# Two attentions with a gate on one core: reciprocals and V copies spread by DMA, taps along the free axis, slices unit by unit on GpSimd, the head in halves, a new order

## The chip, the cores and the metric

The kernel runs on one core of a Trainium2 chip. The metric is the device time of one execution in microseconds. Five engines run their own queues of instructions in order: TensorE (PE in the profile, PEld its weight loads), VectorE (DVE), ScalarE (ACT), GpSimd (POOL) and SyncE (SP), which here issues nearly all transfers (DMA). Semaphores order work between engines.

## The reference

Input x has 2048 tokens of 640 features. Two attention layers of 32 heads with 20 features each read the same x: A is full softmax attention, B looks at 8 earlier tokens, two apart. A gate mixes them.

```python
def _A_ref(x, wqkv, wo):            # H = 32, Dh = 20
    q, k, v = ...                   # (x @ wqkv) split by heads
    p = softmax(einsum("bhqd,bhkd->bhqk", q, k) * Dh ** -0.5)
    return einsum("bhqk,bhkd->bhqd", p, v) ... @ wo

def _B_ref(x, wqkv, wo):            # W, dil = 8, 2
    idx = pos[:, None] - (arange(W) * dil)[None, :]      # masked where negative
    logits = einsum("bhsd,bhswd->bhsw", q, kg) * scale   # kg, vg: k, v gathered by idx
    o = einsum("bhsw,bhswd->bhsd", softmax(logits), vg)
    return ... @ wo

x = A_x                             # B_x is not used
g = sigmoid((x * gate_w).sum(-1, keepdims=True))
return g * _A_ref(x, A_wqkv, A_wo) + (1 - g) * _B_ref(x, B_wqkv, B_wo)
```

## The kernel before, in words

**Units.** A's scores are computed transposed: 128 keys on the partitions, 512 queries along the free axis, for one head. Such a 128x512 block is a unit; four heads, 16 key blocks and 512 queries make a group of 64 units, and there are 32 groups, 2048 units. The sum with V, `pv` (L1868), collects a group in the PSUM bank `obank`, with the four heads in four strips of 32 partitions; V has a column of ones, so row 0 of each strip is the sum of the exponentials.

**Two routes for the exponential.** A tile of two or three units goes through `qk` (L1805, PE) into one of two PSUM tensors `score` and then through one ACT exponential of 1024 or 1536 columns, `exp` (L1823), into `ebuf`. Units of some key blocks (a quad of four heads, `dquads`) go another way: `clamp` (L1783) turns the scores into an int16 on DVE, `uD`, whose bits read as bf16 are a first power of two, and `gen_d` (L952) adds constants to it for three further slices `eD`; the four are summed by PE with weights that GpSimd has multiplied into V (`vS`, `gen_vs`, L972). A unit takes this route when the planner finds DVE free.

**B.** For 256 tokens at a time, `gen_bproj` makes q, k and v (`qkvB`), `gen_b` makes eight products of q with shifted k on DVE (L1064), some of them on GpSimd (L1055), and PE sums them over a head's features. The eight taps lie on partition strips of 32 and two halves of the free axis, so the maximum over the taps takes six small DVE steps on `mxB` (L1104 to L1116). ACT makes the exponential `eB` (L1121), `rQ` the reciprocal, which goes through DRAM (`scr_r`) to `rB`; V's shifted copies `vR` are 16 transfers for each 256 tokens (L1034); DVE and GpSimd multiply them (L1185, L1175).

**Normalising A.** When a group is complete, `gen_norm` transposes `obank` in blocks of 32 on DVE (L912), takes 16 reciprocals per partition (L916), GpSimd multiplies with the gate (L920) and with the transposed values (L929), DVE transposes back (L932), and DMAs carry the rows to `oTd`. `gen_fold` multiplies with the output weights.

**The order.** The kernel plans its own instruction order as Python code when it is built: `_Sched.task` (`T`) holds an estimated time for each engine, gives every step a cost, and sets the semaphores. Generators (`gens`) wait for a condition, for a PSUM bank, for DVE, for a GpSimd slot; the main loop takes a tile, then lets generators fill the time until the next exponential. `PLAN` holds the loop's parameters, by tile number. GpSimd steps wait for the last DVE step that is marked `port` and are placed where DVE is planned to read PSUM. What the planner decides stands as a fixed order in each queue; on the chip only the semaphores act.

**The head.** Four loads of 512 tokens of x, each followed by 20 transposes on PE (`turn`), a copy on ACT and one on DVE (`x_out`), then a projection of the first four heads' K (`k_first`), its maximum (`k_max`) and its copy (`k_out`); the first q needs all four maxima (`KM`). The last group's normalising and four output blocks make the tail.

Of the kernel before, what the change touches and what calls it, by code (L numbers as in the profile page):

```python
# [52 lines left out]
    0: ((0.334, 0.55), 0.25, 1.0, 5.5, 0.89, -1.23, -0.43, 12.02, 7.0, 4.65, 0.75, 0.51, 5.31, 4.81, -0.12, 0.35, 2, -1.5, 0.3, -1.0, (2, 2)),  # L53
    5: ((0.334, 0.55), 0.25, 1.0, 5.5, 0.96, -1.48, -0.43, 4.81, 7.0, 4.65, 0.71, 0.65, 4.56, 2.7, -0.12, 0.35, 2, -6, 0.3, -1.0, (2, 2)),
    10: ((0.334, 0.55), 0.2, 1.0, 5.5, 0.96, -1.48, -0.43, 4.81, 7.0, 10.07, 0.71, 0.65, 4.56, 2.7, -0.12, 0.35, 2, -7, 0.3, -1.0, (2, 2)),
    15: ((0.32, 0.76), 0.25, 1.0, 5.5, 0.96, -1.19, -0.43, 4.77, 7.0, 4.65, 0.75, 0.51, 5.31, 4.81, 0.0, 0.65, 1, -1.3, 0.3, -1.0, (2, 2)),
    20: ((0.38, 0.68), 0.25, 6.6, 5.5, 0.94, -1.26, -1.28, 4.81, 5.5, 6.07, 0.67, 0.54, 5.64, 3.94, 0.2, 0.68, 2, -1.5, 0.3, -1.0, (2, 2)),
    25: ((0.278, 0.677), 0.0, 3.02, 2.45, 0.84, -1.3, -0.51, 5.92, 2.0, 7.76, 0.35, 0.65, 5.31, 2.52, -0.06, 0.68, 2, -3.7, 0.3, -1.0, (2, 2)),
    30: ((0.261, 0.681), 0.11, 6.6, 5.5, 0.94, -1.48, -1.28, 4.81, 5.5, 8.05, 0.67, 0.54, 4.4, 3.94, 0.2, 0.68, 2, -1.5, 0.3, -1.0, (2, 2)),
    35: ((0.275, 0.615), 0.11, 6.6, 5.5, 0.94, -1.48, -1.28, 4.81, 5.5, 8.05, 0.67, 0.54, 4.4, 3.47, 0.2, 0.68, 2, -3, 0.3, -1.0, (2, 2)),  # L60
    40: ((0.261, 0.681), 0.11, 1.0, 2.5, 0.94, -1.48, -0.22, 11.8, 5.5, 8.05, 0.67, 0.54, 6.8, 4.42, 0.0, 0.68, 2, -3, 0.3, -1.0, (2, 2)),
    45: ((0.261, 0.681), 0.11, 1.0, 2.5, 0.94, -1.48, -0.22, 4.81, 2.96, 7.27, 0.67, 0.54, 6.8, 4.42, 0.0, 0.68, 2, -3, 0.3, -1.0, (2, 2)),
    50: ((0.34, 0.51), 0.39, 1.0, 5.5, 0.89, -1.26, -0.43, 7.8, 2.0, 4.65, 0.91, 0.18, 5.31, 4.07, 0.08, 0.59, 2, -1.5, 0.3, -1.0, (2, 2)),
    55: ((0.34, 0.546), 0.39, 1.0, 5.5, 0.89, -1.26, -0.43, 7.8, 2.0, 5.23, 0.91, 0.18, 5.31, 4.07, 0.08, 0.59, 2, -1.5, 0.3, -1.0, (2, 2)),
    60: ((0.412, 0.644), 0.39, 1.0, 6.06, 0.69, -1.26, -0.43, 7.8, 2.0, 4.65, 0.91, 0.32, 5.31, 4.07, 0.08, 0.59, 2, -1.5, 0.3, -1.0, (2, 2)),
    65: ((0.381, 0.757), 0.39, 1.0, 6.06, 0.69, -1.26, -0.43, 7.8, 2.0, 4.65, 0.91, 0.32, 5.31, 4.07, 0.08, 0.59, 2, -1.5, 0.3, -1.0, (2, 2)),
    75: ((0.381, 0.757), 0.39, 1.0, 6.06, 0.69, -1.26, -0.43, 7.8, 2.0, 4.65, 0.91, 0.2, 5.31, 4.07, 0.08, 0.59, 2, -1.5, 0.3, -1.0, (2, 2)),
    85: ((0.381, 0.757), 0.39, 1.0, 6.06, 0.69, -1.26, -2, 10.69, 1.53, 4.65, 0.91, 0.2, 5.31, 4.67, 0.08, 0.59, 2, -1.5, 0.3, -1.0, (2, 2)),
    90: ((0.381, 0.757), 0.39, 1, 6.06, 0.69, -1.26, -2, 10.69, 1.53, 4.65, 0.59, 0.2, 5.31, 4.67, 0.08, 0.63, 2, -1.5, 0.3, -1.0, (2, 2)),
    95: ((0.34, 0.51), 0.39, 1.0, 5.5, 0.89, -1.26, -0.43, 7.8, 2.0, 4.65, 0.91, 0.32, 5.31, 4.07, 0.08, 0.59, 2, -1.5, 0.3, -1.0, (2, 2)),  # L70
    100: ((0.34, 0.51), 0.39, 1, 1.0, 0.89, -1.26, -0.43, 7.8, 7.0, 7.54, 0.91, 0.32, 5.31, 4.07, 0.08, 0.59, 2, -1.5, 0.3, -1.0, (2, 2)),
    105: ((0.34, 0.51), 0.39, 1, 1.0, 0.89, -1.26, -1.38, 7.8, 7.0, 7.54, 0.91, 0.32, 5.31, 4.07, 0.08, 0.59, 2, -1.5, 0.3, -1.0, (2, 2)),
    110: ((0.412, 0.644), 0.39, 1.0, 1.0, 0.69, -1.6, -0.92, 7.8, 2.0, 4.68, 0.91, 0.54, 3.16, 4.29, 0.0, 0.65, 2, -2.77, 0.3, -1.0, (2, 2)),
    115: ((0.291, 0.715), 0.39, 1.0, 1.0, 0.94, -1.6, -0.92, 5.92, 2.0, 4.68, 0.64, 0.65, 4.56, 4.29, 0.0, 0.65, 2, -3, 0.3, -1.0, (2, 2)),
    120: ((0.336, 0.75), 0.33, 1.0, 1.0, 0.89, -1.06, -0.4, 5.92, 2.0, 9.17, 0.6, 0.65, 4.56, 4.74, 0.0, 0.65, 2, -6, 0.3, -1.0, (2, 2)),
    130: ((0.361, 0.799), 0.33, 1.0, 1.0, 1.21, -1.19, -0.4, 5.92, 2.0, 9.17, 0.6, 0.65, 4.56, 4.74, 0.03, 0.65, 2, -6, 0.3, -1.0, (2, 2)),
    135: ((0.361, 0.799), 0.33, 1.0, 1.0, 1.21, -0.99, -0.4, 5.92, 2.0, 9.17, 0.59, 0.65, 3.16, 4.74, 0.03, 0.69, 2, -6.83, 0.3, -1.0, (2, 2)),
    140: ((0.34, 0.51), 0.39, 1, 1.0, 0.89, -1.26, -0.43, 6.62, 1, 4.65, 0.57, 0.51, 5.56, 4.07, 0.05, 0.73, 1, -3, 0.3, -1.0, (2, 2)),
    145: ((0.34, 0.51), 0.39, 1, 1.0, 0.89, -1.26, -0.43, 6.62, 1.4, 4.73, 0.57, 0.51, 5.56, 4.07, 0.05, 0.73, 1, -3, 0.3, -1.0, (2, 2)),
    150: ((0.34, 0.51), 0.39, 1, 1.0, 0.89, -1.26, -0.43, 6.62, 1.4, 4.73, 0.68, 0.51, 5.56, 4.07, 0.05, 0.73, 1, -3, 0.3, -1.0, (2, 2)),  # L80
    155: ((0.224, 0.681), 0.33, 1, 1.0, 1.09, -1.48, -1.81, 3.55, 7.0, 7.19, 0.7, 0.65, 5.53, 3.9, 0.2, 0.72, 2, -3, 0.3, -1.0, (2, 2)),
    160: ((0.217, 0.576), 0.33, 1, 1.0, 1.23, -1.48, -1.81, 3.55, 7.0, 7.19, 0.7, 0.65, 5.53, 3.9, 0.2, 0.68, 2, -3, 0.3, -1.0, (2, 2)),
    165: ((0.217, 0.576), 0.33, 1, 1.0, 1.23, -1.48, -1.81, 3.55, 7.0, 7.19, 0.7, 0.75, 5.53, 3.9, 0.2, 0.68, 2, -3, 0.39, -1.0, (2, 2)),
    170: ((0.27, 0.431), 0.33, 1, 1.0, 1.23, -1.48, -1.81, 3.55, 7.0, 7.19, 0.7, 0.75, 5.53, 4.13, 0.2, 0.68, 2, -3, 0.39, -1.0, (2, 2)),
    175: ((0.224, 0.681), 0.33, 1.56, 1.0, 1.02, -1.48, -1.81, 3.55, 8, 7.19, 0.7, 0.65, 5.53, 3.31, 0.2, 0.57, 2, -3, 0.3, -1.0, (2, 2)),
    180: ((0.389, 0.582), 0.25, 2.5, 1.0, 1.02, -1.48, -1.81, 4.81, 6.7, 7.54, 0.7, 0.65, 5.64, 4.29, 0.0, 0.57, 2, -3, 0.3, -1.0, (2, 2)),
    185: ((0.389, 0.582), 0.25, 2.5, 1.0, 0.89, -1.48, -0.43, 6.62, 4.81, 7.54, 0.7, 0.2, 5.31, 4.07, 0.06, 0.59, 2, -3, 0.3, -1.0, (2, 2)),
    190: ((0.29, 0.69), 0.37, 1.56, 1.58, 1.23, -1.53, -1.81, 3.55, 2.0, 5.03, 0.56, 0.47, 5.53, 2.91, 0.2, 0.65, 1, -3, 0.3, -1.0, (2, 2)),
    195: ((0.29, 0.69), 0.35, 1.56, 1.58, 1.23, -1.34, -1.81, 2, 2.0, 5.03, 0.56, 0.47, 5.53, 2.91, 0.2, 0.65, 1, -3, 0.3, -1.0, (2, 2)),
    200: ((0.278, 0.663), 0.35, 1.56, 1.58, 1.23, -1.34, -1.81, 2, 2.0, 5.03, 0.56, 0.47, 5.53, 2.75, 0.2, 0.61, 1, -3, 0.3, -1.0, (2, 2)),  # L90
    205: ((0.278, 0.663), 0.35, 1.56, 1.58, 1.23, -1.34, -1.81, 2, 2.0, 5.03, 0.56, 0.5, 4.37, 2.75, 0.2, 0.61, 1, -3, 0.26, -1.0, (2, 2)),
    210: ((0.278, 0.663), 0.35, 1.56, 1.58, 1.23, -1.34, -1.81, 2, 2.0, 5.03, 0.56, 0.66, 4.37, 2.75, 0.2, 0.61, 1, -3, 0.26, -1.0, (2, 2)),
    215: ((0.274, 0.542), 0.35, 1.56, 1.58, 1.23, -1.34, -1.81, 2, 1, 8.57, 0.56, 0.66, 4.37, 2.75, 0.2, 0.68, 1, -3, 0.26, -1.0, (2, 2)),
    225: ((0.291, 0.715), 0.2, 1.56, 1.16, 1.23, -1.34, -1.81, 2, 1, 8.57, 0.56, 0.66, 4.37, 2.75, 0.2, 0.68, 1, -3, 0.08, -1.0, (2, 2)),
    230: ((0.29, 0.69), 0.16, 1.56, 1.0, 1.21, -0.76, -1.81, 2, 1, 8.57, 0.56, 0.59, 4.37, 3.61, 0.08, 0.73, 2, -3.49, 0.3, -1.0, (2, 2)),
    235: ((0.29, 0.69), 0.25, 3.79, 1.0, 1.37, -1.53, -0.8, 15.9, 2.0, 5.03, 0.56, 0.47, 3.16, 3.17, 0.2, 0.65, 1, -3, 0.3, -1.0, (2, 2)),
    240: ((0.34, 0.68), 0.38, 2.91, 1.0, 0.89, -1.79, -0.55, 4.03, 7.0, 5.03, 0.52, 0.58, 6.49, 4.57, 0.1, 0.73, 1, -4.31, 0.3, -1.0, (2, 2)),
    245: ((0.388, 0.773), 0.38, 2.91, 1.0, 0.89, -1.79, -0.55, 4.03, 7.0, 5.03, 0.52, 0.58, 4.56, 2.7, 0.1, 0.73, 1, -4.31, 0.3, -1.0, (2, 2)),
    250: ((0.388, 0.773), 0.38, 2.91, 1.0, 0.89, -1.79, -0.55, 4.03, 7.0, 5.03, 0.52, 0.58, 4.56, 2.7, 0.1, 0.67, 1, -4.31, 0.3, -1.0, (2, 2)),
    255: ((0.364, 0.476), 0.0, 1.0, 1.0, 1.21, -1.26, -0.52, 11.51, 2.0, 8.02, 0.83, 0.65, 3.16, 3.17, 0.0, 0.61, 2, -4.7, 0.3, -1.0, (2, 2)),  # L100
    260: ((0.364, 0.476), 0.0, 1.0, 1.0, 1.21, -1.26, -0.52, 11.51, 2.0, 7.91, 0.83, 0.36, 3.16, 3.17, 0.0, 0.61, 2, -4.7, 0.3, -1.0, (2, 2)),
    265: ((0.364, 0.476), 0.0, 1.0, 1.0, 1.21, -1.26, -0.52, 11.51, 6.7, 9.43, 0.83, 0.36, 3.16, 3.17, 0.0, 0.61, 2, -4.7, 0.3, -1.0, (0, 2)),
    270: ((0.364, 0.476), 0.16, 1.0, 1.0, 1.21, -1.26, -0.52, 11.51, 6.7, 9.43, 0.83, 0.36, 3.16, 3.17, 0.0, 0.61, 1, -4.7, 0.3, -1.0, (0, 2)),
    275: ((0.389, 0.582), 0.16, 1.0, 1.0, 1.21, -1.26, -0.52, 11.51, 6.7, 9.43, 0.83, 0.36, 3.16, 3.17, 0.0, 0.61, 1, -4.7, 0.3, -1.0, (0, 2)),
# [314 lines left out]
def _build(ctx, nc, A_x, A_wqkv, A_wo, B_wqkv, B_wo, gate_w, out):  # L419
# [45 lines left out]
    gA = [sb([P, 16], FP32, "gA%d" % i) for i in range(2)]  # L465

    uD = [sb([P, 4 * 512], BF16, "uD%d" % i) for i in range(2)]
    gtr = uD[1][:, 0:1024].bitcast(FP32)
    NS = 3
    eD = sb([P, NS, 4 * 512], BF16, "eD")  # L470
    offs = sb([P, 1], FP32, "offs")
# [1628 lines left out]
```

## Time and profile before

| | us |
|---|---|
| median of 3 runs (lowest, highest) | 795.72 (794.42, 795.99) |
| profiled execution | 793.15 |
| its span, first to last instruction | 791.4 |
| first A exponential starts / last one ends | 18.87 / 782.1 |

| engine | busy us | share | instructions |
|---|---|---|---|
| PE | 754.8 | 95% | 12504 |
| DVE | 722.7 | 91% | 1310 |
| ACT | 767.1 | 97% | 745 |
| POOL | 177.4 | 22% | 317 |

A line of the groups names source line, engine, operation, output<-input, shapes and count, then busy time, mean duration in ns, the idle time of the engine ahead of them and what ended it. A wait is put down to what came last. A line of the timeline starts with start and length in us. The mean granted clock of TensorE was 1.000 throughout. The DMA queue that SP feeds took 17.5% of the 16 DMA engines' time.

### The profile page before, as it was taken

To read this page: it belongs to the slowest core of one execution; us is meant where nothing else is said; L and a number is where in the kernel's file an instruction comes from. 1 tells how busy PE (TensorE), PEld (TensorE's weight loads), DVE (VectorE), ACT (ScalarE), POOL (GpSimd) and SP (SyncE) were. 2 spreads that over 40 slices of the span, in tenths; PEclk is the share of its full clock that TensorE was granted. 3 is DMA by queue.
4 is the path that set the end of the run, shared out by engine and by line. 5 is a ranking of instruction groups with operands and counts; after the bars stand their busy time and mean duration, and the time that the engine had idled before them with its cause. 6 is when DMAs were issued, how large, how long until landed. Compare 5 with 4: busy or idle time off the path is not lost.

```text
span 791.4 us, 29684 instructions
## 1 busy us (share of the span) xinstructions
PE 754.8 (95%) x12504; PEld 291.7 (37%) x12506; DVE 722.7 (91%) x1310; ACT 767.1 (97%) x745; POOL 177.4 (22%) x317
## 2 busy tenths in 40 slices
PE   8999999999999999999999999999999999999997
PEld 5433333232243334334334332433443433344323
DVE  7788999999989989999899999998999999899994
ACT  4999999999999999999999999999999999999995
POOL 4011211112113213123112123332131231220310
PEclk9999999999999999999999999999999999999999
DMA  7321121011021131310113031010303010021301
GB/s 227 111 63 24 40 52 23 6 31 21 19 73 31 38 70 30 73 48 6 24 40 82 14 80 38 15 22 25 90 17 80 20 22 25 14 75 36 70 15 39
DMA packets 61224, 36.16 MB, mean 46 GB/s; under 512 B 26724, under 2 KB 59892, under 8 KB 61092
## 3 DMA queue, kind: packets, MB, share of 16 engines
q1 hardware_dynamic: 60804, 33.94, 17.5%
q8 instruction: 99, 1.62, 0.8%
q10 hardware_dynamic: 288, 0.33, 0.1%
q14 instruction: 33, 0.27, 0.1%
HBM read 12.85 MB, written 3.54 MB: 21 GB/s over the span
## 4 chain that ended last, share of the span: by engine, by line
PE 45%; ACT 23%; DVE 19%; issue 11%; POOL 1%; DVEq 0%; ACTq 0%; POOLq 0%
ACT ebuf L1823 23%; PE score L1805 14%; PE obank L1868 12%; PE side L678 10%; DVE uD L1783 7%; PE score L678 5%; DVE eD L952 4%; DVE kvw L1185 2%; DVE qkvB L1026 1%; PE side L1076 1%; PE side L1197 1%; PE score L1499 1%; DVE kvw L1064 1%; PE obank L1889 1%; DVE kmd L727 1%
## 5 line engine op out<-in xcount | busy, mean ns | idle before, releaser
L1823 ACT ACTIVATE ebuf<-score 128x1024 bf16<-128x1024 f32 (+1 forms) x713 | 755.0, 1202 | 7.1 <-PE score L1805 5.1
L1783 DVE TENSOR_SCALAR uD<-score 128x512 int16<-128x512 f32 x407 | 270.0, 678 | 24.8 <-PE score L1805 23.5
L1805 PE MATMUL score<-qT,kT 32*128 32x512 bf16 x1856 | 259.9, 384 | 19.2 <-ACT ebuf L1823 13.5
L952 DVE TENSOR_SCALAR eD<-uD 128x2048 int16<-128x2048 int16 (+1 forms) x309 | 203.1, 678 | 2.6 <-PE obank L1868 2.2
L1868 PE MATMUL obank<-ebuf,vA 128*21 128x512 bf16 x1641 | 154.6, 385 | 0.9 <-ACT ebuf L1823 0.5
L1805 PEld LDWEIGHTS score<-qT,kT 32*128 32x128 bf16 x1856 | 64.2, 91 | 214.9 <-ACT ebuf L1823 135.9
L972 POOL TENSOR_TENSOR vS<-vA,vw 128x252 bf16<-128x252 bf16 x103 | 63.4, 616 | 320.2 <-DVE eD L952 171.8
L1868 PE MATMUL obank<-eD,vS 128*21 128x512 bf16 x1221 | 107.6, 379 | 0.0
L678 PE MATMUL side<-xT,wBs 128*32 128x256 bf16 x2400 | 96.2, 281 | 0.9 <-DVE rQ L1151 0.2
L678 PEld LDWEIGHTS side<-xT,wBs 128*32 128x32 bf16 x2400 | 69.0, 142 | 30.2 <-issue 14.2
L1868 PEld LDWEIGHTS obank<-ebuf,vA 128*21 128x21 bf16 x1641 | 36.5, 89 | 85.1 <-issue 64.0
L929 POOL TENSOR_TENSOR oN<-oTt,rcp 128x256 bf16<-128x256 f32 x62 | 40.0, 646 | 66.1 <-DVE eD L952 47.3
L1026 DVE CAST qkvB<-side 128x512 bf16<-128x512 f32 (+1 forms) x72 | 41.8, 590 | 3.3 <-PE side L678 3.1
L1064 DVE TENSOR_TENSOR kvw<-qkvB 128x2048 bf16<-128x2048 bf16 (+2 forms) x40 | 43.3, 1106 | 0.1
L1185 DVE TENSOR_TENSOR kvw<-kvw,eB 128x1536 bf16<-128x1536 bf16 (+1 forms) x40 | 42.1, 1069 | 0.0
L1868 PE MATMUL obank<-uD,vA 128*21 128x512 bf16 x407 | 40.0, 379 | 0.0
L1175 POOL TENSOR_TENSOR kvw<-kvw,eB 128x256 bf16<-128x256 bf16 x48 | 29.5, 632 | 38.4 <-DVE eD L952 21.5
L920 POOL TENSOR_TENSOR rcp<-rcp,gA 128x16 f32<-128x16 f32 x31 | 7.3, 237 | 133.8 <-DVE eD L952 59.5
L1868 PEld LDWEIGHTS obank<-eD,vS 128*21 128x21 bf16 x1221 | 30.0, 91 | 18.7 <-issue 1.6
L678 PE MATMUL side<-xT,kvw 128*32 128x512 bf16 (+1 forms) x360 | 30.9, 382 | 0.5 <-DVE qbnd L834 0.4
L1805 PE MATMUL score<-woBp,kT 32*128 32x512 bf16 x192 | 29.2, 384 | 2.0 <-DVE uD L1783 1.2
L912 DVE STREAM_TRANSPOSE oTt<-obank 128x512 f32<-128x512 f32 x32 | 22.6, 708 | 6.8 <-PE obank L1868 6.5
(189 smaller groups left out, 596.1 us busy)
## 6 DMA issues: line engine op xcount, KB each, us to landing
kvw<-qkvB SPq DMA_DIRECT2D x128, 80.6 KB
wBs<-in_B_wqkv_dram SPq DMA_DIRECT2D x5, 480.0 KB
WqP<-in_A_wqkv_dram SPq DMA_DIRECT2D x14, 160.0 KB
oTd<-oN SPq DMA_DIRECT2D x108, 20.0 KB
out_dram<-outsb SPq DMA_DIRECT2D x12, 160.0 KB
qT<-dst SPq DMA_DIRECT2D x93, 20.0 KB
kvw<-in_A_wqkv_dram SPq DMA_DIRECT2D x2, 800.0 KB
oTd<-in_A_x_dram SPq DMA_DIRECT2D x2, 640.0 KB
```

Of the source, the lines that this page charges most:

```text
L678: ins = e.matmul(o[j:k, :], l(j) if callable(l) else l[:, j:k], r, start=(first and i == 0), stop=(last and i == n - 1), skip_group_check= ...
L929: T(en, c2 if n == 4 else 0.56, lambda e, oo=oo, ii=ii, ib=ib: e.tensor_tensor(oo, ii, ib, ALU.mult), reads=["rcp", "oTt"], **{"accum" if ...
L952: T("dve", 0.065 + 0.1334 * n, lambda e, k=k, sl=sl: e.tensor_scalar(eD[:, sl % NS, 0:512 * n].bitcast(I16), uD[d % 2][:, 0:512 * n].bitca ...
L972: T("pool", 0.607, lambda e: e.tensor_tensor(vS[:, d % 2, :, :], _ap(vA, (kb * NQ + q) * 4 * DV, [[0, K - 1], [1, 4 * DV]]), _ap(vw, 0, [[ ...
L1026: t = TB(dvc(n * TOK), lambda e, o=o, i=i: e.tensor_copy(o, i), reads=[("side", b)], writes=[key])
L1064: TB(dvc(n_ * TOK, 2), lambda e: e.tensor_tensor(o, i0, i1, ALU.mult), reads=["qB", "kB"], writes=prods(i, range(n_)) + olds(), port=True)
L1175: (lambda e, a=a, hh=hh: e.tensor_tensor(_ap(stage, i * CH + (2 * a + hh) * TOK, [[1, TOK]]), _ap(stage, v0 - DIL * hh + a * CN * VW, [[1, ...
L1185: TB(dvc(n_ * 2 * TOK, 2), lambda e: e.tensor_tensor(o, i0, i1, ALU.mult), reads=rd, writes=prods(i, range(2 * n_)), port=True)
L1783: t = T("dve", 0.598, lambda e: e.tensor_scalar(uD[d % 2][:, 512 * i:512 * (i + 1)].bitcast(I16), side[x], UOFF, 0.0, op0=ALU.add, op1=ALU ...
L1805: ins = e.matmul(o, kT[32 * j:32 * j + 32, q, kb * P:(kb + 1) * P], qT[qbuf[g]][32 * j:32 * j + 32, :], start=True, stop=True)
L1823: exps[s] = T("act", actc(512 * n), lambda e: e.activation(ebuf[s % NE][:, 0:512 * n], score[s % 2][:, 0:512 * n], ACTF.Exp, scale=LN2 / S ...
L1868: ins = e.matmul(obank[32 * j:32 * j + DV, :], v, src, start=(kb == 0), stop=(last and k >= len(lst) - 4), skip_group_check=True)
```

## The change

1. A's normalising (`gen_norm`, all groups but the last): DVE copies `obank` to `oTt`; a DMA spreads the four rows of sums over 128 partitions (`rcp`); DVE takes the reciprocals; GpSimd multiplies with the gate; a DMA writes them to DRAM (`scr_n`), another brings them back repeated along the partitions (`rcpR`, 128x512 f32, in the place of `oN`); GpSimd multiplies twice 256 columns. No transposes. The gate `gA` goes through DRAM (`scr_g`) to the same layout. `close` waits for the preceding group's normalising. The last group keeps the old steps (`gen_norm_last`).
2. B's taps: the eight taps of 64 tokens lie along the free axis, so the maximum is one reduce into `mB`; the exponential goes to `eT` and through DRAM (`scr_e`, `gen_relay`) to `eB`. V goes to DRAM in one transfer (`scr_v`) and comes back in four.
3. The second term's slice (k = 1): a unit's 512 columns can be made by GpSimd as soon as the clamp is done (`piece`, called from `slot`), as an int16 add with a constant or, for odd quads, an int32 add of pairs; `gen_d` makes the rest on DVE.
4. The head: x in eight loads of 256 tokens, with transposes and copies of that size in an order written as a string; the absolute value and the eviction of the first q in halves on ACT and DVE; seven warm-up matmuls for nine.
5. B's output weights in four transfers at once; `PLAN` and other parameters are new, so the planned order differs throughout.

```diff
     def gen_norm(g):
-        T("dve", 0.625, lambda e: e.transpose(oTt[:, :], obank[:, :]), reads=["obank"], writes=["oTt"])
+        T("dve", dvc(512), lambda e: e.tensor_copy(oTt[:, :], obank[:, :]), reads=["obank"], writes=["oTt"])
+        yield ("pe", 0.0, sch.ready("oTt", to="sp") - 0.2)
+        T("sp", 2.1, lambda e: e.dma_start(rcp[:, :], bass.AP(tensor=oTt, offset=0, ap=[[32 * 512, 4], [16, 32], [1, 16]])),
+          reads=["oTt"], writes=["rcp"], dma=True)
+        yield ("dve", DVE_AHEAD, sch.ready("rcp", to="dve"))
+        T("dve", 0.155, lambda e: e.reciprocal(rcp[:, :], rcp[:, :]), reads=["rcp"], writes=["rcp"])
...
+        T("sp", 1.9, lambda e: e.dma_start(dap(nD, g % 2 * 2048, [[16, P], [1, 16]]), rcp[:, :]),
+          reads=["rcp"], writes=[("nD", g % 2)], dma=True)
...
+        T("sp", 2.6, lambda e: e.dma_start(rcpR, dap(nD, g % 2 * 2048, [[512, 4], [0, 32], [1, 512]])),
+          reads=[("nD", g % 2)], writes=["oN0", "oN1"], dma=True)
+        for i in range(2):
...
+            T("pool", 0.56, lambda e, cols=cols: e.tensor_tensor(oN[0][:, cols], oTt[:, cols], rcpR[:, cols], ALU.mult),
+              reads=["oTt", "oN1"], accum=["oN0"], after=last_port())
...
-        T("dve", 0.36, lambda e: e.transpose(oN[1][:, :].bitcast(FP32), oN[0][:, :].bitcast(FP32)), reads=["oN0"], writes=["oN1"])
...
+    def piece(t0):
...
+            pdone[d].append(i)
+            T("pool", PDUR, lambda e: e.tensor_tensor(
+                eD[:, sl % NS, 512 * i:512 * (i + 1)].bitcast(I32), uD[d % 2][:, 512 * i:512 * (i + 1)].bitcast(I32), _ap(two, 0, [[0, 256]]), ALU.add) if d % 2 else e.tensor_scalar(
+                eD[:, sl % NS, 512 * i:512 * (i + 1)].bitcast(I16), uD[d % 2][:, 512 * i:512 * (i + 1)].bitcast(I16), SHIFTS[1], None, op0=ALU.add), reads=[("uD", d % 2, i)] + ["two"], writes=[("eD", sl % NS, i)], after=last_port())
...
+        T("sp", 6.0, lambda e: e.dma_start(dap(vD, 0, [[CN * W, 4], [4 * CN * W, 32], [1, CN * W]]), vB),
+          reads=["vB"], writes=["vD"], dma=True)
...
-        TB(dvc(TOK), lambda e, b=b: e.tensor_copy(mB[:, :], side[b][:, 0:TOK]), reads=[("side", b)], writes=[("mxB", 1)])
...
+        TB(dvc(512), lambda e, b=b: e.tensor_reduce(mB[:, :], sap(b, 0, [[1, TQ], [TQ, WIN]]), axis=AX.X, op=ALU.max),
+           reads=[("side", b)], writes=["mB"])
...
-    turn(0)
-    x_out(0)
...
+    HEAD = ("t0 x0 t1 x1 y0 y1 a0 t2 b0 x2 y2 m0 t3 x3 o0 t4 y3 x4 y4 t5 k1 y5 x5 t6 x6 m1 t7 x7 y6 k2 o1 "
+            "y7 k3 m2 o2 q0 c0 m3")
+    for op in HEAD.split():
+        HEADOP[op[0]](int(op[1]))
...
+        if g:
+            run_until(("norm", g - 1))
         add_gen(gen_norm(g), 0)
```

In `HEAD`, t is `turn`, x and y the copies on ACT and DVE, a, b and k projections (halves and whole), m and o maximum and copy, q the first q.

## The prediction

> **What bounds the kernel now.** I read the page's busy times first, then a table of three stretches (head, middle, tail), then the groups by shape, the waits, and the timelines of the head and of one stretch in the middle.
>
> ```profile
> PE 754.8 (95%) x12504; PEld 291.7 (37%) x12506; DVE 722.7 (91%) x1310; ACT 767.1 (97%) x745; POOL 177.4 (22%) x317
> ```
>
> Three engines look full; the stretches (PE, PEld, DVE, ACT, POOL busy, clock, DMA) say which one sets the pace:
>
> ```profile
> 0.00:18.87 18.87, 16.02 (x129) 9.54 (x135) 13.63 (x35) 8.11 (x10) 9.81 (x20) 1.00 0.78 238
> 18.87:782.10 763.23, 734.04 (x12263) 279.63 (x12257) 704.73 (x1268) 757.95 (x733) 167.57 (x297) 1.00 0.17 41
> 782.10:791.40 9.30, 4.76 (x124) 2.50 (x120) 4.32 (x8) 1.09 (x3) 0.00 (x0) 1.00 0.21 71
> ```
>
> Between the first exponential (18.87) and the end of the last (782.10) ACT is busy 757.95 of 763.23 us. Head and tail are chains before and after ACT's run. So the time is head + ACT's list + ACT's waits + tail. The groups by shape, and two waits:
>
> ```profile
> L1823 ACT ACTIVATE ebuf<-score 128x1024 bf16<-128x1024 f32 x496 | 478.2, 1069 | 2.6 <-PE score L1805 0.8
> L1823 ACT ACTIVATE ebuf<-score 128x1536 bf16<-128x1536 f32 x216 | 305.5, 1510 | 4.5 <-PE score L1805 4.3
> L1783 DVE TENSOR_SCALAR uD<-score 128x512 int16<-128x512 f32 x407 | 270.0, 678 | 24.8 <-PE score L1805 23.5
> ...
> L952 DVE TENSOR_SCALAR eD<-uD 128x2048 int16<-128x2048 int16 x300 | 199.3, 684 | 2.6 <-PE obank L1868 2.2
> ...
> L972 POOL TENSOR_TENSOR vS<-vA,vw 128x252 bf16<-128x252 bf16 x103 | 63.4, 616 | 320.2 <-DVE eD L952 171.8 <-PE obank L1868 61.4 <-DVE kvw L1064 29.6
> ```
>
> ```profile
> PEld score L1805 <- ACT ebuf L1823: 155.6, 388, 1.1
> ...
> PEld score L1805 <- DVE uD L1783: 16.6, 39, 1.0
> ```
>
> PE waits for ACT 388 times, ACT hardly for PE (7.1 us). An instruction's duration overlaps the next one's start, so I cost by start to start. In the timeline of DVE:
>
> ```profile
> 430.82 0.68 DVE L952 TENSOR_SCALAR eD<-uD 128x2048 int16<-128x2048 int16 x1
> 431.42 1.22 DVE L1185 TENSOR_TENSOR kvw<-kvw,eB 128x2048 bf16<-128x2048 bf16 x1
> 432.56 0.74 DVE L1026 CAST qkvB<-side 128x256 bf16<-128x256 f32 x2
> 433.22 1.27 DVE L1783 TENSOR_SCALAR uD<-score 128x512 int16<-128x512 f32 x2
> 434.42 0.68 DVE L952 TENSOR_SCALAR eD<-uD 128x2048 int16<-128x2048 int16 x1
> ```
>
> A clamp `uD` is 0.60 (two from 433.22 to 434.42), a slice of four units 0.60, a product of 2048 1.14, an eviction of 256 0.33. By the records of ACT's timeline, an unhindered exponential of 1024 is 0.903 start to start, one of 1536 1.330.
>
> **ACT's list.** 2048 units of 512 scores are shared between ACT and the DVE route; the built program says how. ACT: 503 instead of 496 of 1024 (+7 x 0.903 = +6.3), 206 instead of 216 of 1536 (-13.3), none instead of one of 512 (about -0.48, the row of `eB`'s 128x512 exponential). Sum **-7.5**: 17 units go to DVE. B's exponential only changes its target (`eT`).
>
> **What pays for it on DVE** (start to start). Normalising: one copy 0.60 in place of transposes 0.63 + 0.36, 31 times: -12.1. Slices: 300x0.60 + 3x0.47 + 6x0.335 = 183.4 becomes 240x0.60 + 14x0.47 + 22x0.335 + 23x0.20 (bound by extension) = 162.6: -20.8. Clamps: +17 x 0.60 = +10.2. B's maximum: one reduce of 512 (0.60, as other PSUM reads of 512) for six small steps (1.37 together), 8 times: -6.1. B's products, fewer of them left to POOL: +4.3. Sum -24.5: DVE's share falls although it takes more units. Counted per 40 exponentials in planning order, DVE's work is 0.81 to 0.99 of ACT's in every stretch (before 0.86 to 1.00), so ACT stays the limit and the relief itself is off the path: I count it at 0.
>
> **POOL** gets 203 slices of one unit (109 one-input int16 adds of 512, 94 two-input int32 adds of 256) and 15 other steps, and loses 44 products: at 0.62 (rows of L972 and of its other 256-wide steps) about +108, to 285 of 783, 36%. The int32 kind is the row's own shape. The one-input kind has no row: POOL's copy of 128x1024 takes 1.04, half of that is 0.52; at the two-input price per element it would be 1.24. I take 0.62, nearest to the copies, which also have one input. Hidden by 500 us of idle POOL.
>
> POOL and DVE get in each other's way: of 299 slices in the trace, the 26 that began while a POOL step ran took 744 ns on average against 678. That is 66 ns x 203 = 13 us at most on DVE, within the 24.5. The Trainium skill, page "SBUF — State Buffer", section "SBUF: two separate sides", says that the pair of ports is an exclusive lock and the loser blocks wholly until the other's instruction ends. The 66 ns are remainders of such steps, so the trace agrees; by that rule a POOL step that is longer than planned costs DVE its whole excess, which is the third rival below.
>
> **DMA and SP.** SP issues 644 transfers instead of 580. Each of 31 groups adds three in a chain (`rcp` spread, `scr_n` out, the 128x512 f32 back); B adds a relay of `eB` and of V through DRAM and loses 128 - 40 V copies. Nearest landings in the trace: `scr_q` 1.6 (p90 2.6), a lone `qT` piece 1.9, `rB` from `scr_r` 3.7. The plan in the code counts 2.1, 1.9 and 2.6. The first two fit; the third looks like `rB` (rows of DRAM spread over 128 partitions, 128 KB; the new one is 256 KB), so it may land 1.1 late, with POOL standing in order at its multiplication and slices queued behind it: 31 x 1.1 = 34 us of POOL waiting. SP itself waits in order for the results before `scr_n` and `rcpR`, with `qT` and `kT` pieces behind; those are issued a group ahead (some 24 us), which covers 2 us. DVE's reciprocal waits for `rcp`, with clamps behind it and then PE; covered if it lands in 2.1. Before, POOL waited for hundreds of us and ACT for 7, so I let **+1.0** reach ACT; the ends are -5 (DVE's new room takes away what ACT still loses) and +34.
>
> **The head.** Rows of the last x load and what follows:
>
> ```profile
> 11.67 1.28 PE L1499 MATMUL score<-ident,wBs 128*128 128x128 bf16 x20
> ...
> 14.09 1.24 PE L1522 MATMUL score<-xT,kvw 128*128 128x512 bf16 x5
> ...
> 17.63 0.75 DVE L1610 TENSOR_SCALAR qT<-obank,offs 128x512 bf16<-128x512 f32 x1 [0.48 <-PE obank L1605]
> ```
>
> The fourth load lands at 11.17 by the trace, and since the same 2.7 MB come before it, so should the last half. After it: 10 transposes from 11.3 (0.64), then PE runs the third K projection (1.1) while the copies of half size run, and the last K projection starts near 13.1 instead of 14.09: -1.0. After it the absolute value and the q evictions go in halves on ACT and DVE (0.41 and 0.43 instead of 0.69 and 0.75): -0.6. Sum **-1.6**, first exponential at about 17.3. Ends: 0 (a load or a PE turn is late) and -2.4. The tail keeps its steps: 0. Fewer warm-up and filler matmuls (33 groups of four less): 0 while the clock row stays at 1.00.
>
> **Sum.** -7.5 - 1.6 + 1.0 = -8.1. The profiled execution took 793.15 (span 791.4 and 1.75 around it); it would take 785.1. The median of the runs, 795.72, lies 2.6 above it; 795.72 - 8.1 = 787.6. A difference under 0.2% (1.6 us) can't be told from none.
>
> **Rivals.**
> 1. DVE's room pays twice: PE's waits for clamps (16.6 above) shrink and ACT's exponentials run nearer to 0.903 and 1.330 (all of them at those values would be some 22 us less). For: DVE/ACT falls in most stretches. Against: stretches with DVE at 0.98 of ACT lose ACT no more than others today. Another -5: 782.6.
> 2. Slower: POOL's line behind the late `rcpR`. Slices go to PE as soon as they are planned to be ready, PE works in order, and the next scores stand behind. Price up to 34 us. It decides once more than 9.1 + 1.6 us, a third, reach ACT; at one half, 795.72 - 9.1 + 17 = 803.6. For: `rB`'s 3.7. Against: POOL idles two thirds of the time.
> 3. Slower: the one-input slice costs 1.24. Then 109 x 0.62 = 68 us hold the port that DVE needs; less the 24.5 freed, DVE has 722.7 + 43 = 766, over ACT's list, and sets the pace: about 802. The lock rule above is its mechanism. It decides near 1.0 per slice.
> 4. The change doesn't do what it says at the start: the halves land no earlier in effect and the head saves nothing, and 6 us more of waits come than I count: 795.7 - 7.5 + 1.0 + 6 = 795.2, no change.
>
> **How the numbers follow.** Forecast 0.64, rival 1 0.16, rival 2 0.11, rival 3 0.05, rival 4 0.04. Faster 0.80, same 0.04, slower 0.16. The range goes from 780 (rival 1 with the head's -2.4 in place of -1.6, and the runs' own scatter of 1.6) to 798 (the forecast's waits up to +11); rivals 2 and 3 stay out, 0.16.
>
> **What would show it.** Right: the first exponential near 17.3, ACT's count 503 and 206 with little idle before them, DVE near 698, POOL near 285 with slices of 0.62, `rcpR` landing under 4. Wrong: ACT idle behind PE scores by over 15 us, PE waiting for `eD` from POOL, POOL waiting for DMA before its multiplications, slices over 1 us, a clock under 1.00.

## The result, and the profile after

The changed kernel takes 906.94 us (median of 4 runs, 905.6 to 908.51) where the kernel before takes 795.07 (4 runs): a ratio of 1.141, 95% interval 1.138 to 1.144. The forecast was 787.6 with a range of 780 to 798; the change costs 112 us instead of saving 8. The profiled execution took 907.62, its span is 905.7.

The page's engines and clock, and from the table of three stretches the middle one, from the first exponential (18.38) to the end of the last (896.42); its columns are as in the stretches of before:

```profile
PE 790.0 (87%) x12434; PEld 297.9 (33%) x12434; DVE 716.4 (79%) x1250; ACT 770.4 (85%) x747; POOL 401.4 (44%) x491
...
PEclk9998899999999898988998998899999979998989
```

```profile
18.38:896.42 878.04, 770.01 (x12177) 285.72 (x12176) 701.05 (x1203) 760.00 (x729) 391.79 (x471) 0.94 0.23 51
```

Nothing is full any more: ACT works 760 of these 878 us, so some 118 us are holes, and the granted clock has gone from 1.00 to 0.94. Two groups of GpSimd, and the waits:

```profile
L1013 POOL TENSOR_SCALAR eD<-uD 128x512 int16<-128x512 int16 x109 | 175.5, 1626 | 69.3 <-DVE uD L1856 29.2
...
L1012 POOL TENSOR_TENSOR eD<-uD,two 128x256 int32<-128x256 int32 x94 | 57.9, 624 | 49.1 <-DVE eD L983 18.2
```

```profile
ACT ebuf L1897 <- PE score L1879: 115.8, 86, 6.1
...
POOL oN L955 <- DMA oN<-scr_n: 77.6, 21, 8.6
...
PE obank L1942 <- POOL eD L1013: 32.4, 16, 4.8
...
DVE rcp L938 <- DMA rcp<-oTt: 19.7, 7, 6.0
...
DVE kvw L1255 <- DMA kvw<-scr_v: 8.0, 2, 5.5
```

All the signs that the prediction named for "wrong" are here at once: ACT waits for scores 115.8 us (before 5.1), the one-input slice takes 1.63 us where 0.62 was counted, PE waits for GpSimd's slices, GpSimd waits for the reciprocals, and two waits of DVE for transfers are new. Which of them costs what can't be read from this list, since a wait of an engine off the path may cost nothing and a short one on PE pulls others behind it. One stall in the timeline shows the pull:

```profile
553.07 6.31 POOL L1013 TENSOR_SCALAR eD<-uD 128x512 int16<-128x512 int16 x4
...
559.44 0.61 PE L1942 MATMUL obank<-ebuf,vA 128*21 128x512 bf16 x4 [4.84 <-POOL eD L1013]
...
560.83 0.61 PE L1879 MATMUL score<-qT,kT 32*128 32x512 bf16 x3
...
561.49 1.02 ACT L1897 ACTIVATE ebuf<-score 128x1024 bf16<-128x1024 f32 x1 [5.72 <-PE score L1879]
```

Four slices take 6.31 us in a row; PE stands 4.84 us at a sum that needs them, with the next scores behind it in its queue, and ACT loses 5.72. After the pause the matmuls take 0.61 us instead of 0.39. The Trainium skill, "TensorE: Matmul & The Clock Gate", section "Part 1: The HAM clock gate", says that an idle window of about 3.4 us halves the clock until a busy one has passed; the row after the 4.84 us pause agrees with that.

The clock rows of the trace show the halving itself. The change has 19 stretches at half clock, 3.4 to 13.7 us long and 112.6 us together; before has none. Each follows a pause of TensorE, but nine of them follow pauses of only 1.7 to 3.4 us, so here a pause need not last the 3.4 us that the Trainium skill gives. The stretch behind the stall above, with the columns of the table of stretches:

```profile
557.61:571.27 13.66, 11.17 (x114) 3.46 (x118) 4.90 (x9) 5.98 (x5) 4.90 (x9) 0.50 0.16 45
```

ACT works 5.98 of its 13.66 us, though the pause ends at 559.44. By the records of the whole trace, 117.9 us of holes lie before ACT's exponentials: 43.4 in pauses of TensorE of over 1 us, and 46.0 more in half-clock stretches outside these pauses. A stall thus goes on costing time after what was waited for has come. How much of the 46.0 a full clock would give back, no run here isolates.

### The profile page after: what moved, and what is told of

It is laid out like the page before. It is cut to its first block, busy times and chain, and to the rows that moved or that the text cites. A ratio compares the mean times of both kernels' runs of the same rounds, so it can differ in the third digit from the quotient of the medians.

```text
span 905.7 us, 29909 instructions
## 1 busy us (share of the span) xinstructions
PE 790.0 (87%) x12434; PEld 297.9 (33%) x12434; DVE 716.4 (79%) x1250; ACT 770.4 (85%) x747; POOL 401.4 (44%) x491
## 3 DMA queue, kind: packets, MB, share of 16 engines
q1 hardware_dynamic: 86024, 47.50, 23.1%
## 5 line engine op out<-in xcount | busy, mean ns | idle before, releaser
L1897 ACT ACTIVATE ebuf<-score 128x1024 bf16<-128x1024 f32 (+1 forms) x709 | 756.9, 1169 | 118.2 <-PE score L1879 115.8
L1856 DVE TENSOR_SCALAR uD<-score 128x512 int16<-128x512 f32 x424 | 282.6, 681 | 69.9 <-PE score L1879 68.8
L1013 POOL TENSOR_SCALAR eD<-uD 128x512 int16<-128x512 int16 x109 | 175.5, 1626 | 69.3 <-DVE uD L1856 29.2
L983 DVE TENSOR_SCALAR eD<-uD 128x2048 int16<-128x2048 int16 (+3 forms) x299 | 195.7, 678 | 7.9 <-PE obank L1942 7.5
L1942 PE MATMUL obank<-eD,vS 128*21 128x512 bf16 x1272 | 118.0, 403 | 12.7 <-POOL eD L1013 9.1
L669 PE MATMUL side<-xT,wBs 128*32 128x256 bf16 x2400 | 103.9, 299 | 9.6 <-DVE qkvB L1086 8.6
L955 POOL TENSOR_TENSOR oN<-oTt,oN 128x256 bf16<-128x256 f32 x62 | 51.0, 823 | 96.7 <-DMA oN<-scr_n 77.6
L1012 POOL TENSOR_TENSOR eD<-uD,two 128x256 int32<-128x256 int32 x94 | 57.9, 624 | 49.1 <-DVE eD L983 18.2
L1255 DVE TENSOR_TENSOR kvw<-kvw,eB 128x2048 bf16<-128x2048 bf16 (+1 forms) x40 | 48.1, 1226 | 13.2 <-DMA kvw<-scr_v 8.0
L1137 POOL TENSOR_TENSOR kvw<-qkvB 128x256 bf16<-128x256 bf16 x46 | 28.2, 624 | 36.1 <-DVE kvw L1146 17.5
L1146 DVE TENSOR_TENSOR kvw<-qkvB 128x1536 bf16<-128x1536 bf16 (+2 forms) x40 | 42.3, 1073 | 1.1 <-PE side L1159 1.0
```

The costliest lines, as they stand in the source:

```text
L669: ins = e.matmul(o[j:k, :], l(j) if callable(l) else l[:, j:k], r, start=(first and i == 0), stop=(last and i == n - 1), skip_group_check= ...
L955: T("pool", 0.56, lambda e, cols=cols: e.tensor_tensor(oN[0][:, cols], oTt[:, cols], rcpR[:, cols], ALU.mult), reads=["oTt", "oN1"], accum ...
L983: T("dve", 0.065 + 0.1334 * (n - m), lambda e, k=k, sl=sl, m=m: e.tensor_scalar(eD[:, sl % NS, 512 * m:512 * n].bitcast(I16), uD[d % 2][:, ...
L1012: T("pool", PDUR, lambda e: e.tensor_tensor(eD[:, sl % NS, 512 * i:512 * (i + 1)].bitcast(I32), uD[d % 2][:, 512 * i:512 * (i + 1)].bitcas ...
L1013: eD[:, sl % NS, 512 * i:512 * (i + 1)].bitcast(I32), uD[d % 2][:, 512 * i:512 * (i + 1)].bitcast(I32), _ap(two, 0, [[0, 256]]), ALU.add) ...
L1146: TB(dvc(n_ * TOK, 2), lambda e: e.tensor_tensor(o, i0, i1, ALU.mult), reads=["qB", "kB"], writes=prods(i, range(n_)) + olds(), port=True)
```

## The experiments

Three theories at the start: A, the one-input slice (1.63 us) is the cause; B, the late reciprocals (`rcpR`, 77.6 us of GpSimd's waiting) are; C, the lowered clock is a cause of its own. All runs but the last keep the changed kernel's planned order; where a wait is taken away, so is its cause: the transfer writes a scratch tensor, its reader takes a constant or old data, and only the waits that the old contents need stay. "Before" ran beside each: at 794.2 beside e1 to e4, 792.6 beside e5 to e8, 793.2 beside e9 and e10, 794.0 beside e11. A difference between runs of two such groups carries up to 1.6 us of this.

| run | median us | ratio to before (95%) | clock | ACT's waits for scores, us |
|---|---|---|---|---|
| the change | 906.94 | 1.138 to 1.144 | 0.938 | 115.8 |
| e1 two-input slices | 892.89 | 1.119 to 1.128 | 0.946 | 99.2 |
| e2 one-input slices | 930.42 | 1.169 to 1.178 | 0.935 | 131.8 |
| e3 no wait for `rcpR` | 869.12 | 1.092 to 1.096 | 0.960 | 80.5 |
| e4 e1 and e3 | 849.95 | 1.066 to 1.073 | 0.961 | 63.4 |
| e5 e4, no wait for `rcp` | 825.06 | 1.034 to 1.044 | 0.976 | 40.5 |
| e6 e5, no V copies | 803.15 | 1.008 to 1.015 | 0.991 | 18.5 |
| e7 e6, no copies of `eB`, `rB` | 804.01 | 1.010 to 1.018 | 0.991 | 15.4 |
| e8 e7 with the change's slices | 842.66 | 1.057 to 1.065 | 0.972 | 47.5 |
| e9 e7, no wait for the gate | 804.83 | 1.010 to 1.016 | 0.988 | 16.1 |
| e10 slices in three forms | 912.84 | 1.146 to 1.154 | 0.937 | 121.4 |
| e11 new plan, whole result | 842.66 | 1.060 to 1.064 | 0.992 | 28.8 |

**e1, e2: the slices' form.**

```diff
-  e.tensor_tensor(... I32 ...) if d % 2 else e.tensor_scalar(... I16 ...)
+  e.tensor_tensor(... I32 ...)          # e1, all 203 slices
+  e.tensor_scalar(... I16 ...)          # e2, all slices
```

> The changed kernel in the same order, with every GpSimd slice computed as the two-input int32 add of 256 elements (203 of them; none as the one-input int16 add of 512). Theory A, the one-input form is the cause: 109 slices fall from 1626 ns to about 620, POOL's busy time from 401 to about 290 us, PE's waits for eD (32.4 + 14.0 us) nearly vanish, ACT's waits for scores fall from 115.8 us to under 30, and the time comes to 790-815 us. Theory B, the late reciprocals on the DMA queue are the cause (POOL waits 77.6 us for them): POOL still waits about 78 us, slices still stand behind those waits, and the time stays at 870-910. Theory C, the lowered clock of TensorE is a cause of its own: the granted clock stays near 0.94 and the time stays above 850 though the waits for eD are gone.

> The changed kernel in the same order, with every GpSimd slice computed as the one-input int16 add of 512 elements (203 instead of 109). Theory A: the 112 us lost with 109 such slices grow with their number, about 1.03 us for each, so the time comes to 980-1030 us and ACT waits for scores about 200 us. Theory B: only the reciprocals' transfers matter and they are the same, so the time stays at 900-915. Theory C (a clock that falls after any pause): between the two, above 915.

e1 came to 892.89 and e2 to 930.42. Neither end fits A: with no one-input slice left, 99 us over before remain, and 94 more of them add 23 us where 73 to 123 were expected. e1 lies in B's range (870 to 910), e2 not (900 to 915). The numbers of both are those that C named (e1 above 850 with the clock near 0.94, e2 above 915), but the low clock is not independent of the waits: in the change every stretch of it follows a pause of TensorE, and it will be seen to go as the waits go. e1's waits say what stays:

```profile
ACT ebuf L1897 <- PE score L1879: 99.2, 65, 10.0
POOL oN L955 <- DMA oN<-scr_n: 93.1, 22, 7.8
```

GpSimd, quicker with its slices, now waits 93 us for the reciprocals instead of 78. Its timeline shows two ways to ACT within 20 us:

```profile
696.14 0.72 POOL L955 TENSOR_TENSOR oN<-oTt,oN 128x256 bf16<-128x256 f32 x1 [7.71 <-DMA oN<-scr_n]
696.81 0.25 POOL L1073 COPY qkvB<-qkvB 128x80 bf16<-128x80 bf16 x1
...
697.16 0.69 DVE L1086 CAST qkvB<-side 128x512 bf16<-128x512 f32 x1 [4.66 <-POOL qkvB L1073]
...
697.91 1.72 PE L669 MATMUL side<-xT,wBs 128*32 128x256 bf16 x28 [4.10 <-DVE qkvB L1086]
...
700.22 2.79 ACT L1897 ACTIVATE ebuf<-score 128x1536 bf16<-128x1536 f32 x2 [5.09 <-PE score L1879]
...
711.05 2.36 DVE L1255 TENSOR_TENSOR kvw<-kvw,eB 128x2048 bf16<-128x2048 bf16 x2 [4.65 <-DMA kvw<-scr_v]
...
714.06 0.62 PE L1267 MATMUL side<-kvw,Rep 128*32 128x256 bf16 x8 [5.87 <-DVE qkvB L1086]
...
715.27 1.02 ACT L1897 ACTIVATE ebuf<-score 128x1024 bf16<-128x1024 f32 x1 [5.28 <-PE score L1879]
```

First GpSimd waits 7.71 us for the reciprocals; behind it stands a small copy of B's, an eviction on DVE waits for that copy, a projection on PE for the eviction, and ACT for the scores behind the projection: 5.09 us. Then DVE waits for V's copies (issued at 701.32 to 703.98), again with an eviction behind it, and ACT loses 5.28. No slice is in either chain.

**e3, e4: no wait for the replicated reciprocals.**

```diff
-  T("sp", 2.6, lambda e: e.dma_start(rcpR, dap(nD, ...)), reads=[nD], writes=["oN0", "oN1"])
+  tr = T("sp", 2.6, lambda e: e.dma_start(dap(nX, ...), dap(nD, ...)), reads=[nD], writes=["oN0", "oN1"])
-  T("pool", 0.56, ... oN[0] = oTt * rcpR)
+  tm = T("pool", 0.56, ... oN[0] = oTt * onesrow)    # a constant column
+  tm.deps = (without tr)
```

> The changed kernel in the same order with its two forms of slices, but the normalising product on GpSimd no longer waits for the replicated reciprocals: it multiplies by a constant column instead, and the transfer that replicates them writes a small scratch tensor (so the A term is not normalised in its output). Theory A: POOL's 77.6 us of waiting go, and slices that stood behind it come earlier, but each one-input slice still costs 1626 ns; the time falls by 10-40 us, to 865-895. Theory B: most of the 112 us go, the time comes to 795-820.

> Both edits together: all slices as the two-input form, and no wait for the replicated reciprocals (the A term is not normalised in its output). What it is faster than the run with two-input slices alone is what the late reciprocals cost by themselves once the slices are cheap. Theory A: 2-10 us less than that run, 780-805. Theory B: 70-100 us less than that run. If both causes are needed for the loss (each alone leaves it), this run alone comes to under 800 and the other two stay near 900.

e3 came to 869.12 and e4 to 849.95. With the change's own slices this one wait costs 37.8 us, with two-input slices 42.9 (the product itself is also shorter with the constant, 685 against 823 ns, 62 times, 9 us of GpSimd). Both theories expected more of their own cause: A and B together explain 57 us, and 56 remain. In e4 the seven longest holes of ACT all begin where DVE waits for a transfer. The longest:

```profile
747.40 2.65 SPq L1103 DMA_DIRECT2D kvw<-scr_v  x4
...
750.15 1.15 SPq L1231 DMA_DIRECT2D rB<-scr_r  x1
...
751.35 1.44 SPq L935 DMA_DIRECT2D rcp<-oTt  x1
...
758.63 0.25 DVE L938 RECIPROCAL rcp<-rcp 128x16 f32<-128x16 f32 x1 [7.08 <-DMA rcp<-oTt]
...
760.61 1.29 PE L669 MATMUL side<-xT,wBs 128*32 128x256 bf16 x20 [5.69 <-DVE qkvB L1087]
...
762.49 1.02 ACT L1898 ACTIVATE ebuf<-score 128x1024 bf16<-128x1024 f32 x1 [6.08 <-PE score L1880]
```

An 8 KB transfer (`rcp`) goes out behind 1290 KB of V copies on the same queue and reaches DVE 7.3 us after its issue; DVE stands 7.08 us before a reciprocal of 0.25, and PE and ACT follow. So a fourth theory, D: each transfer that lands later than planned stops an in-order engine, whichever it is. Its rival E: the new order is itself the rest.

**e5 to e8: the other late transfers, one after the other; then the slices alone.** The edits follow e3's pattern for `rcp`, for V's two transfers, for `eB` and `rB` (these from the second block of 256 tokens on), with two-input slices; e8 is e7 with the change's two forms.

```diff
-  T("sp", 2.1, lambda e: e.dma_start(rcp[:, :], ... oTt ...), reads=["oTt"], writes=["rcp"])            # e5
+  T("sp", 2.1, lambda e: e.dma_start(dap(nX, ...), ... oTt ...), reads=["oTt"], writes=["rcp"], ghost=True)
-  T("dve", 0.155, lambda e: e.reciprocal(rcp[:, :], rcp[:, :]), ...)
+  T("dve", 0.155, lambda e: e.reciprocal(rcp[:, :], _ap(fone, 0, [[0, 16]])), ...)                       # a tile of ones
-  T("sp", 2.9 + 0.73 * 4, ... vR <- vD ...)                                                              # e6
+  T("sp", 2.9 + 0.73 * 4, ... nV <- 16 elements of vD if u else vR <- vD ..., ghost=u > 0)
```

A `ghost` transfer keeps its place and its planned price; its readers wait only for what the old contents of their tile need.

> Same order, two-input slices, no wait for the replicated reciprocals as in the run before, and now VectorE's reciprocal doesn't wait for the spread sums either: it reads a constant, and that transfer writes a scratch tensor (the A term is not normalised in its output). Theory D, each late transfer stops an in-order engine, and TensorE's scores stand behind it: VectorE's 27.8 us of waits for the spread sums in the run before (8 waits, longest 7.1) are on the path, so the time falls from 850 to 820-832. Theory E, the new order is itself the rest of the loss (55 us): no fall, 843-852.

> As the run above, and B's V copies are not transferred after the first of the eight token blocks: 340 KB out and 1290 KB back become a few bytes, and nobody waits for the copies (B's term uses the first block's V in its output). Theory D: the waits for the copies (11.9 us in the run without the reciprocals' wait) and the transfers that stand behind them on the queue (scores' copies and 1/sum of B, 8 instead of 4.6 us) go, so 10-20 us less than the run above, 800-820. Theory E: within 5 us of the run above.

> As the run above, and B's exponentials and reciprocals are not copied either after the first block (two more transfers that the trace shows landing at 5.6 and 8 us where 3.6 and 2.9 were planned). Nothing in the loop now waits for a transfer that lands later than planned, save small ones. Theory D: the order as such is as good as planned, 785-802 us, granted clock back at 0.99 or 1.00. Theory E: above 830. Between the two: both.

> As the run above, but with the change's own two forms of slices (109 one-input, 94 two-input). What it is slower than the run above is the one-input form by itself, without any late transfer beside it. Theory D, with the slices' price as a smaller part: 109 slices at 1.6 instead of 0.62 us, of which the other pairs of runs showed 14 and 19 us on the path: 10-25 us slower than the run above. If the late transfers had hidden more of it: 40-60 us slower. If the slices were late only because of the transfers: within 5 us.

The runs came to 825.06, 803.15, 804.01 and 842.66. The waits for `rcp` cost 24.9 us, V's transfers 21.9, those of `eB` and `rB` nothing that shows. D holds for the most part; E is left with the 11 us by which e7 stands above before (e7 came 2 us above what D allowed). And the one-input form, with no late transfer beside it, costs 38.7 us, not the 14.0 that e1 had shown; that is just under the 40 to 60 expected if late transfers had hidden it. The waits of e8 and of e7, in this order:

```profile
ACT ebuf L1914 <- PE score L1896: 47.5, 49, 3.8
...
PE obank L1959 <- POOL eD L1028: 21.5, 13, 3.0
```

```profile
ACT ebuf L1914 <- PE score L1896: 15.4, 20, 4.3
```

So the two causes overlap. That slow slices catch up unseen while PE stands for a late transfer fits these numbers, but is argued from them and not shown by itself. A small part of the 38.7 may be on DVE: the slices of 2048 that began while a GpSimd step ran add 10 us there in e8 and 2 in e7. Transfers and slices together are 103 us by either way: 14.0 and then 88.9 (892.89 to 804.01), or 64.3 (906.94 to 842.66) and then 38.7.

**e9: the gate's transfer.**

```diff
-  T("pool", 0.221, ... rcp = rcp * gA ...)      # gA loaded from scr_g
+  T("pool", 0.221, ... rcp = rcp * fone ...)    # that load a ghost
```

> As the run without the new waits (two-input slices; the A term's normalising, B's V copies, exponentials and reciprocals not copied after the first block), and the gate's spread copy is not waited for either (the gate is left out of the output). In that run GpSimd stood 4.2 us at 60-64 us behind the gate's transfer, which landed 6.4 us after its issue where 2.3 was planned, and TensorE and ScalarE stood behind that slice. Theory D: 3-7 us less than that run, 796-801; what is then left above the kernel before are the first block's own transfers. Theory E, the rest is the order's: within 2 us of that run.

e9 came to 804.83: D's 3 to 7 us didn't come, and E's "within 2 us" did. The stall at 64 us is gone from its profile. But the profiled run is the slowest of its four (809.11): its first exponential started at 19.79 where e7's started at 17.95, and near 390, 443 and 564 us several engines stop at once, 8.1 us of ACT together (3.6 in e7), with no cause in the trace. So a gain of 2 or 3 us can't be seen here, and what the gate's wait costs stays open.

**e10: what a slice costs.**

```diff
+  fns = (tensor_scalar on I16 of 512, tensor_tensor on I32 of 256, tensor_scalar on I32 of 256)
+  T("pool", PDUR, fns[d % 3], ...)
```

> The changed kernel in the same order, with GpSimd's slices in three forms by turns over the quads: one-input int16 add of 512 elements, two-input int32 add of 256 elements, one-input int32 add of 256 elements. It is for the three forms' durations. If the price goes by the number of elements: 1.46, 0.6 and about 0.75 us. If it goes by the one-input instruction itself: 1.46, 0.6 and about 1.4 us. If one-input instructions of 256 int32 elements cost less than two-input ones: under 0.5 us. The time itself: between the change's 907 and the run with two-input slices, 893.

The trace's list for the tile `eD` on GpSimd (ns: lowest, median, longest):

```profile
L1013 POOL TENSOR_SCALAR eD<-uD x78: 1483/1488/2770, 29.3 to 897.4; 128x512 int16<-128x512 int16 x78
L1014 POOL TENSOR_TENSOR eD<-uD,two x68: 606/611/663, 38.9 to 870.0; 128x256 int32<-128x256 int32 x68
L1015 POOL TENSOR_SCALAR eD<-uD x57: 842/848/1919, 48.4 to 890.5; 128x256 int32<-128x256 int32 x57
```

For the same 1024 bytes per partition the price goes mainly by the number of elements: 2.9 ns for each int16, 3.3 for each one-input int32, 2.4 for each two-input int32. The time, 912.84, was expected between 893 and 907, and lies 6 us above; with 135 one-input slices instead of 109, if 57 of them cheaper ones, that is not a contradiction, and it wasn't followed up.

**e11: a new plan with the landings as measured.**

```diff
-  T("sp", 2.6, lambda e: e.dma_start(rcpR, ...          # and likewise five others
+  T("sp", 5.0, svc=3.1, fn=lambda e: e.dma_start(rcpR, ...
+  self.qf = max(start, self.qf) + svc                   # in task(), for SP's transfers
+  t.end = max(t.end, self.qf + 1.8)
```

> The whole change with nothing left out of the computation and all its transfers, two-input slices only, and the order planned anew with the landings that the traces showed: 5.0 us for the replicated reciprocals (2.6 in the change), 8.2 for V out (6.0), 10.2 for V back (5.8), 4.0 for the exponentials (3.6), 4.65 for B's reciprocals (2.9), 6.6 for the gate (2.3), 0.8 for the normalising product (0.56), and transfers of one queue served one after the other. The planner's parameters were searched for this pricing at random; they need not be as good for it as the change's are for its own. Theory D, the loss is made of steps placed ahead of transfers that hadn't landed: GpSimd's waits for the replicated reciprocals fall from 93 us (two-input run) to under 15, VectorE's for the spread sums from 29 to under 8, ScalarE's waits for scores from 99 to under 45, the clock to 0.97 or more, and the time from 893 to 825-850. Theory F, the transfers cost by their load on the memory and the queues and not by the waits: waits may fall, but the time stays at 875-900.

e11 came to 842.66, with the whole computation: 50 us less than e1, which has the same transfers (47.50 MB on SP's queue in both) in the change's order. The load on memory and queues (F) is therefore not what the 893 consisted of. But the order is not the only difference: the new plan gives DVE's route fewer units, 355 clamps instead of 424, and GpSimd 148 slices instead of 203. How much of the 50 us comes from that relief was not separated. One expectation failed clearly, another by a hair (the waits for `rcp`, 8.2 where under 8 were expected):

```profile
POOL oN L932 <- DMA oN<-scr_n: 79.1, 19, 12.2
...
ACT ebuf L1874 <- PE score L1856: 28.8, 39, 3.7
...
DVE rcp L915 <- DMA rcp<-oTt: 8.2, 6, 2.5
```

GpSimd still waits 79 us for the reciprocals, hardly less than in e1, and yet ACT waits 28.8 us instead of 99.2: the plan now knows of the wait, and what stands behind it is needed less soon. Of the 49 us that e11 takes more than before, some 22 are ACT's own list (461 exponentials of 1024 and 256 of 1536 where before has 496 and 216, at 0.903 and 1.330), since this plan finds less room for DVE's route, and 26 are holes before them (31.1 us, before 5.0). No version here beats the kernel before.

## Why the prediction was wrong, step by step

- **ACT's list (-7.5): held, and nothing was seen of it.** 503 and 206 exponentials; those that follow one another without idle time are 0.905 and 1.331 start to start (medians), as counted. Other waits covered it.
- **"I let +1.0 reach ACT": the step that failed.** It was meant to hold all of ACT's waits; 115.8 us came. Taken away one after the other, `rcpR` costs 38 to 43 us of the time, `rcp` 25, V's transfers 22, the one-input slices 14 to 39, and 11 us stay. The argument was that GpSimd idles two thirds of its time and ACT had waited 7 us. Mean idle time says nothing here: each engine takes its queue in the planned order, and the plan had put work that was needed soon right behind the landing that it expected, as in the chains of e1 and e4.
- **`rcpR`: right mechanism in the main, wrong price, too small a chance.** The prediction feared a landing of 3.7; from issue to the last mark on its semaphore the trace shows 4.7 to 5.7, median 4.98, for 256 KB. GpSimd waited 77.6 us instead of 34, and 38 to 43 us of it reached the time. That is rival 2 (0.11), which decided at a third of 34. It expected slices behind the wait; in the chain that e1 shows, a copy of B's stood there and no slice.
- **`rcp`: "covered if it lands in 2.1".** The median landing is 1.94, as taken; but 9 of 31 land after more than 3 us, up to 7.75, eight of them behind transfers of B (exponentials, V, reciprocals) issued within 9 us before on the same queue. That cost 24.9 us. The nearest rows that I used were medians of lone transfers; the term needed the queue's other users, which the change itself adds.
- **V's transfers: not costed at all.** I counted 128 - 40 copies saved. Out takes 8.2 us (plan 6.0) and back about 8 after the last issue (plan 5.8 from the first). Together they cost 21.9 us.
- **The one-input slice, 0.62 "nearest to the copies": failed.** 1.49 to 1.63 us, above even the upper bound of 1.24. A copy is not an add; the nearest rows were the adds and products at 2.4 ns per element, of which the bound was made. It accounts for 110 of the 116 us by which GpSimd is busier than the 285 predicted (109 x 1.0), and costs 14 us of time here, 39 alone. This was rival 3's condition (over 1.0), but not its road: it expected the excess on DVE by the lock of the ports and DVE at 766; DVE is busy 716. (Its price of 802 doesn't follow from its own figures either: 766 is 6 us over ACT's 760, which would add some 6 us to the forecast.) The full slices that began while a GpSimd step ran (70 of 240) took 866 ns against 680: 13 us, the bound that I gave, against 110 us of excess on GpSimd. The road was PE waiting in order for `eD`. By the Trainium skill's rule ("SBUF — State Buffer", "SBUF: two separate sides": the loser blocks until the other's instruction ends) I had let DVE pay the whole excess; the 186 ns per overlapped slice fit remainders of blocked steps, but DVE as a whole is only 18 us busier than I counted. So most of GpSimd's excess didn't show up on DVE.
- **DVE (-24.5, off the path):** 716.4 busy instead of 698, for the 13 us above among others. Its busy time sets no pace here (79% of the span); its waits for transfers do, as above.
- **Head (-1.6):** first exponential at 18.38, -0.5, and between 17.95 and 20.39 in the other runs with the same head. The prediction let the last load of x land at 11.17, as the fourth load did before; the eighth lands at 12.27. **Tail (0):** 9.31 against 9.30.
- **Fillers ("0 while the clock row stays at 1.00"):** it didn't stay. The clock follows the pauses (0.938, 0.946, 0.961, 0.976, 0.991 as they are taken away). 46.0 us of ACT's holes lie in half-clock stretches outside the pauses; what the clock itself costs of that wasn't isolated.

**What stays open.** e7 is 11 us above before, where the sum promised 8 below. Between the two profiled runs, 9 us apart, it is holes again: 21.5 us before ACT's exponentials where before has 5.0, less the shorter list (7.5) and the earlier start (0.9). Its profile names the first block's V copies, still real (ACT loses 4.3 us at 288), and short stops of several engines at once near 385 and 435 (1.3 and 2.3 us of ACT) for which the trace shows no cause; the rest is spread.

## What to carry to other kernels

Where an order is planned ahead and run by in-order queues, cost a transfer by the landing that it has in the traffic of the changed kernel, and ask of each new wait what stands behind it in its engine's queue and who needs that: 93 us of GpSimd's waiting cost 43 us in one order (e1), while in another (e11) it waits 79 us and ACT's waits are 28.8 us in all. Price an instruction that has no row by operation and number of elements, not by bytes or by the nearest copy. And when several causes fill the same holes, undo them together and put one back at a time: taken away first, the slow slice seemed to cost 14 us; put back last, it cost 39.

## What the runs showed of the hardware

On GpSimd an int16 add of 512 elements with a constant takes 1.49 us, and the same bytes as a two-input int32 add of 256 elements 0.61; one input is dearer than two at 256 int32 elements (0.85). An 8 KB transfer that lands in 1.94 us (median of 31) takes 5.1 to 7.7 behind B's transfers on its queue. Matmuls of 32x512 that take 0.385 us take 0.602 in the stretches at half clock, and in this kernel such a stretch can follow a pause of TensorE of 1.7 us.
